# A decode step on one core: the last weight matrix in other pieces, and one early read ahead of the closing add

## The chip, the cores and the metric

The kernel runs on one core of a Trainium2 chip. The metric is the time of one execution in microseconds (us), measured on the device; 212.2 us is the median of four runs of the kernel before (212.13 to 212.42). One of these executions, of 212.18 us, was recorded by the hardware profiler, and every view of the profile below is of that one. The engines are TensorE (PE in the profile; PEld is its loading of weights), VectorE (DVE), ScalarE (ACT), GpSimd (POOL) and SyncE (SP). SP issues nearly all transfers from the chip's memory (HBM) into on-chip memory.

## The reference, cut to what matters

Four tokens of width 576 are normalised; the sum of three things is returned: the tokens, an attention over a window of a long cache, and a multi-layer perceptron.

```python
def _A_ref(x, k_cache, v_cache, wq, wo):       # 4 tokens, 32 query heads, 16 key/value heads of 128
    W = min(4096, max(256, Sk // 4))           # Sk = 8192: the last 2048 positions
    q = (x @ wq) ...                           # by heads
    k, v = the last W rows of the caches, each head used by two query heads
    p = softmax((q . k) * Dh ** -0.5)
    return (p @ v) by tokens @ wo              # wo is 4096 x 576

def _B_ref(x, w1, w2, w3, w4):
    ...                                        # hs: a shift over one position, so it adds zeros
    x1 = x + hs
    h2 = gelu(layernorm(x1) @ w3) @ w4         # w3 is 576 x 4608, w4 is 4608 x 576
    return x1 + h2

xn = layernorm(A_x)
return A_x + _A_ref(xn, ...) + _B_ref(xn, ...)
```

The mixer's four shifts each move the only position out of the sequence, so `w1` and `w2` play no part in the result, and the kernel does not load them.

## The kernel before, in words

**Transfers.** `flush_loads` (L497 to L509) hands SP one list in a fixed order: the keys and values of the 16 heads (2 MB each), four parts of `wo`, `w3` after the values of head 2, and at the very end `w4`. Six buffers hold keys and values, and a transfer is issued when one of them comes free. `w4` is issued by `load_w4` (L135) as six transfers. The 4608 rows of `w4` lie on the 128 partitions as 36 rows of 576 numbers on each (`NF` is 36); the two halves of the matrix give the rows 0 to 17 and 18 to 35 (`NFH` is 18). `W4_PIECES` (L133) cuts these 36 rows: [0, 10, 18, 28, 32, 34, 36], which are pieces of 10, 8, 10, 4, 2 and 2 rows. A row on all partitions is 128 x 1152 bytes, 144 KB.

**The loop.** The big loop (L514 to L565) runs over the heads, with VectorE transposing keys, TensorE making scores and multiplying probabilities with values, and a softmax between them. The first three layers of the perceptron's work lie inside the turn of head 7, so `gT`, its activations, are ready long before the end. The order of the work on each engine is the order in which the code is written.

**The sum of outputs.** Every product with `wo` and with `w4` is accumulated in PSUM by `acc_matmuls` (L177). The width of 576 is cut into two halves of 288 columns (`CW`), which go to different rows of one 8-row sum: the weights, `gT` or `op`, are stored with gaps (`OW` is 10 columns, the tokens in columns 1, 3, 5, 7), and a window of 8 columns beginning at column 1 or at column 0 puts the four tokens on the even or on the odd rows. So a row of `w4` costs two matrix multiplications of 288 columns.

**Two sums at the end.** When the list `second` is filled (L592), every other term is accumulated in another PSUM tile, `acc_odd`, at the rows from 32 on (`QD`), and two multiplications to the two sums run at the same time. `mlp_out(lo, hi)` (L483) takes the rows lo to hi of `w4`, two at a time, one for each sum. After the loop come the last heads' values, the pieces 0 and 1 of `w4`, the last part of `wo`, and the pieces 2 and 3. Then `second` is cleared (L602), ScalarE copies `acc_odd` to `odd` in on-chip memory (L604), the pieces 4 and 5 go to `acc` alone (L605, L606), VectorE adds `acc` and `odd` to `fin` (L609) and SP writes `fin` out (L610).

Of the kernel before, what the change touches and what calls it, by code (L numbers as in the profile page):

```python
# [9 lines left out]
ALU = mybir.AluOpType  # L10
AX = mybir.AxisListType
BF16 = mybir.dt.bfloat16
F32 = mybir.dt.float32
# [9 lines left out]
def kernel(  # L23
# [14 lines left out]
    nc = tc.nc  # L38
    P = 128
    B, Sq, D = A_x.shape  # L40
# [8 lines left out]
    NF = F // P  # L49
    NFH = NF // 2  # L50
# [4 lines left out]
    NQD = P // QD  # L55
    NSL = 4
    SC = NC // NSL
    CW = D // 2
    NW = SC * QD
    assert NW == 512 and NSL * NJ == QD and NQ == 2 * NQD * NW and NFH == 18  # L60
    scale = float(Dh) ** -0.5
# [5 lines left out]
    o2 = out.flatten_outer_dims()  # L67
# [14 lines left out]
    const = ctx.enter_context(tc.tile_pool(name="const", bufs=1))  # L82
# [47 lines left out]
        nc.sync.dma_start(out=t[:, KJ * F:], in_=B_w3[KJ * P:D, :].rearrange("r (e f) -> (r e) f", e=2))  # L130
        w_tiles["w3"] = t

    W4_PIECES = [0, 10, NFH, NFH + 10, NFH + 14, NF - 2, NF]  # L133

    def load_w4():  # L135
        t = wp.tile([P, NF, D], BF16, tag="w", name="w4_sb")
        for lo, hi in zip(W4_PIECES, W4_PIECES[1:]):
            e = lo // NFH
# [8 lines left out]
    ident_f = ident_w[:, 0:P]  # L147
# [7 lines left out]
    def cleared(shape, name):  # L155
        t = const.tile(shape, BF16, name=name)
        flat = t[:] if len(shape) == 2 else t[:].rearrange("p a b -> p (a b)")
        flat = flat.bitcast(F32)
        nc.scalar.activation(out=flat, in_=zero[:].bitcast(F32).to_broadcast(list(flat.shape)), func=ACT.Copy)
        return t  # L160
# [2 lines left out]
    ln2T = cleared([P, KJ + 2, QD], "ln2T")  # L163
    ZP = (NSL - 1) * NJ
    qz = cleared([P, ZP + Hkv * 4 * P], "qz")
    OR = 2 * B
    OW = OR + 2
    gT = cleared([P, NF, OW], "gT")
    op = cleared([P, WOR, OW], "op")

    acc = ps_acc.tile([P, CW], F32)
    nc.vector.memset(acc[:], 0.0)
# [2 lines left out]
    second = []  # L175

    def acc_matmuls(terms):  # L177
        for i in range(2):
            for n, (lhsT, rhs) in enumerate(terms):
                to, q, start = (second[0], QD, second[1]) if second and n % 2 else (acc, 0, False)  # L180
                nc.tensor.matmul(out=to[q:q + OR, :], lhsT=lhsT[:, 1 - i:1 - i + OR],  # L181
                                 rhs=rhs[:, i * CW:(i + 1) * CW], start=start, stop=False, skip_group_check=True)
                if start:
                    second[1] = False
# [43 lines left out]
    for kb in range(NQD):  # L228
        nc.vector.tensor_copy(out=sel[:, :, :, kb, :],
                              in_=ident_bf[:].rearrange("p (ib i e) -> p ib e i", ib=2, e=2))  # L230
# [19 lines left out]
    with nc.allow_low_precision("zeros and ones"):  # L250
# [7 lines left out]
                          in_=sel_j[:].unsqueeze(1).to_broadcast([P, NG, NJ]))  # L258
# [7 lines left out]

    idz = const.tile([B, OW], F32)
    nc.gpsimd.memset(idz[:], 0.0)
    nc.gpsimd.tensor_copy(out=idz[:, 1:OR + 1:2], in_=ident_f[0:B, 0:B])
    xsum = xn_f  # L270
    nc.vector.tensor_tensor(out=xsum[:], in0=xn_f[:], in1=x_bf[:], op=ALU.add)
    acc_matmuls([(idz[:], xsum)])
    ln2_bf = part(D, B)
    layernorm(None, ln2_bf, xn_bf)
# [25 lines left out]
    for r in range(2):  # L300
        nc.vector.tensor_copy(out=q_bf[:, r],
                              in_=qT_ps[:, r].rearrange("p u (g x) -> p g u x", g=NQD)[:, :, :, 0:B])
# [101 lines left out]
    def o_sum(h):  # L404
        oT = st.pop(("oT", h))
        v = oT[:].rearrange("p s (g x) -> p (s g) x", g=NQD)[:, :, 0:NJ].rearrange("p g (b r) -> p b r g", r=rep)
        k = h % WOQ
        if k == 0:
            st["on"] = small.tile([P, WOH, B], BF16, tag="on", name="on")
        with nc.allow_low_precision("summed in float32"):  # L410
            nc.vector.reduce_sum(out=st["on"][:, k * rep:(k + 1) * rep, :].rearrange("p r b -> p b r"),  # L411
                                 in_=v, axis=AX.X)
# [12 lines left out]
    def o_pick(h):  # L425
        if h % WOQ < WOQ - 1:
            return
        R = st.pop("R")
        mk = small.tile([P, WOR, WOH, B], BF16, tag="mk")
        nc.vector.tensor_tensor(out=mk[:], in0=R[:],  # L430
                                in1=own[:].unsqueeze(1).unsqueeze(3).to_broadcast([P, WOR, WOH, B]), op=ALU.mult)
        with nc.allow_low_precision("one term is not zero"):
            nc.vector.reduce_sum(out=op[:, :, 1:OR + 1:2], in_=mk[:].rearrange("p i h b -> p i b h"), axis=AX.X)

    def o_proj(h):
        if h % WOQ < WOQ - 1:
            return
        for i in range(0, WOR, 2):
            acc_matmuls([(op[:, i + u, :], wo_tiles[h // WOQ][:, i + u, :]) for u in range(2)])

    G_CHUNKS = [(e, 4 * g, 4) for e in range(2) for g in range(NQD)] + [(e, 16, 2) for e in range(2)]
    xs = const.tile([P, NF, B], F32, name="g_x")
# [31 lines left out]
    def mlp_act():  # L474
        u = const.tile([P, NF, B], F32, name="g_u")
        nc.vector.tensor_tensor(out=u[:], in0=xs[:], in1=xs[:], op=ALU.mult)
        nc.vector.tensor_scalar(out=u[:], in0=u[:], scalar1=GELU_A, scalar2=1.0, op0=ALU.mult, op1=ALU.add)
        nc.vector.tensor_tensor(out=u[:], in0=u[:], in1=xs[:], op=ALU.mult)
        nc.scalar.activation(out=u[:], in_=u[:], func=ACT.Tanh, scale=GELU_C)
        nc.vector.tensor_scalar(out=u[:], in0=u[:], scalar1=0.5, scalar2=0.5, op0=ALU.mult, op1=ALU.add)  # L480
        nc.vector.tensor_tensor(out=gT[:, :, 1:OR + 1:2], in0=u[:], in1=xs[:], op=ALU.mult)

    def mlp_out(lo, hi):  # L483
        w4 = w_tiles["w4"]
        for i in range(lo, hi, 2):
            acc_matmuls([(gT[:, i + u, :], w4[:, i + u, :]) for u in range(2)])


    order = [("K", 0), ("K", 1), ("K", 2)]
# [24 lines left out]
    for t in range(Hkv):  # L514
        hm, hv, hf, hp = t - 1, t - 2, t - 3, t - 4
        for s in range(NSL):
            if s == NSL - 1 and hm >= 0:
                sm_turn(hm)
            n = t * NSL + s + 1
# [3 lines left out]
            if s == 0:  # L523
                if hm >= 0:
                    sm_max(hm)
                if hv >= 0:
                    sm_rec(hv)
                if hp >= 0:
                    o_pick(hp)
                if hf >= 0:  # L530
                    o_scale(hf)
                k_mask(t)
            elif s == 1 and hm >= 0:
                sm_maxT(hm)
            elif s == 2:
                if hm >= 0:
                    sm_sub(hm)
                    sm_exp(hm)
                if hf >= 0:
                    o_sum(hf)  # L540
            elif s == 3 and hm >= 0:
                sm_den(hm)
# [12 lines left out]
            if t == G_AT:  # L555
                if s < 3:
                    mlp_g(s)
                if s > 0:
                    mlp_turn(s - 1)
                if s == NSL - 1:  # L560
                    mlp_act()
# [27 lines left out]
    o_sum(hl - 1)  # L589
    pieces = list(zip(W4_PIECES, W4_PIECES[1:]))  # L590
    acc_odd = ps_acc.tile([P, CW], F32, tag="g", name="acc_odd")
    second += [acc_odd, True]  # L592
    mlp_out(*pieces[0])
    o_turn(hl)
    o_sum(hl)
    o_spread(hl)
    o_pick(hl)
    mlp_out(*pieces[1])
    o_proj(hl)
    mlp_out(*pieces[2])  # L600
    mlp_out(*pieces[3])
    second.clear()  # L602
    odd = const.tile([OR, CW], F32)
    nc.scalar.activation(out=odd[:], in_=acc_odd[QD:QD + OR, :], func=ACT.Copy)  # L604
    for lo, hi in pieces[4:]:  # L605
        mlp_out(lo, hi)  # L606

    fin = const.tile([OR, CW], out.dtype)
    nc.vector.tensor_tensor(out=fin[:], in0=acc[0:OR, :], in1=odd[:], op=ALU.add)  # L609
    nc.sync.dma_start(out=o2.rearrange("b (i n) -> (b i) n", i=2), in_=fin[:])  # L610


# [28 lines left out]
```

## Time and profile before

| What | Value |
|---|---|
| Median of four runs | 212.2 us (212.13 to 212.42) |
| The profiled execution: its time, its span | 212.18 us, 210.4 us |
| TensorE busy, VectorE busy, ScalarE busy | 150.1, 120.3, 33.9 us |
| Moved from HBM, mean rate over the span | 87.17 MB, 414 GB/s |
| Last piece of `w4` landed | 207.04 us |
| Closing add begins | 207.84 us |
| Mean granted TensorE clock | 0.878 of full speed |

Times in the views are counted from the first instruction. The execution's own time is 1.78 us longer than its span. The chain of waits follows the work that ended last back in time, and names at each step what released it; a line of it is the start, the duration, and the engine with the tile and the line. A row of the timeline is a start, a duration, an engine, the line, the operation, and what it writes and reads; brackets hold the idle time before it and what ended that. The table of stretches gives for each stretch its length, the busy time and count of each engine, the granted clock, the mean busy share of the 16 DMA engines, and the rate in GB/s.

### The profile page before, as it was taken

To read this page: it belongs to the slowest core of one execution; us is meant where nothing else is said; L and a number is where in the kernel's file an instruction comes from. 1 tells how busy PE (TensorE), PEld (TensorE's weight loads), DVE (VectorE), ACT (ScalarE), POOL (GpSimd) and SP (SyncE) were. 2 spreads that over 40 slices of the span, in tenths; PEclk is the share of its full clock that TensorE was granted. 3 is DMA by queue.
4 is the path that set the end of the run, shared out by engine and by line. 5 is a ranking of instruction groups with operands and counts; after the bars stand their busy time and mean duration, and the time that the engine had idled before them with its cause. 6 is when DMAs were issued, how large, how long until landed. Compare 5 with 4: busy or idle time off the path is not lost.

```text
span 210.4 us, 2403 instructions
## 1 busy us (share of the span) xinstructions
PE 150.1 (71%) x955; PEld 62.2 (30%) x955; DVE 120.3 (57%) x216; ACT 33.9 (16%) x64; POOL 2.8 (1%) x15
## 2 busy tenths in 40 slices
PE   0294793889393009769799599987883946988974
PEld 0131231224131003214255143343331321443542
DVE  4732999267730082737504879997578391583220
ACT  7603110021111000202012111220211010202300
POOL 4010000000000000000000000000000000000000
PEclk9999699589978555969699969999999795999999
DMA  7999999999999999999999999999999999999991
GB/s 275 424 392 439 427 428 427 433 433 430 433 442 412 436 430 424 439 430 430 430 430 430 433 422 441 424 430 435 421 435 433 427 430 430 436 424 425 425 407 54
DMA packets 6659, 87.32 MB, mean 415 GB/s; under 512 B 748, under 2 KB 760, under 8 KB 1400
## 3 DMA queue, kind: packets, MB, share of 16 engines
q1 hardware_dynamic: 6640, 87.17, 97.4%
q8 instruction: 7, 0.11, 0.2%
q14 instruction: 4, 0.03, 0.0%
q10 hardware_dynamic: 8, 0.00, 0.0%
HBM read 87.17 MB, written 0.00 MB: 414 GB/s over the span
## 4 chain that ended last, share of the span: by engine, by line
DMA 66%; PE 19%; DVE 7%; issue 4%; ACT 1%; POOL 0%; POOLq 0%; SPq 0%; DVEq 0%
DMA vn<-in_A_v_cache_dram 38%; DMA w_sb<-in_B_w_dram 28%; PE S L336 9%; DVE kt L223 3%; PE g_ps L454 2%; PE O L388 2%; PE q_ps L283 2%; PE acc L181 1%; PE oT L401 1%; DMA first<-in_A_x_dram 1%; PE S L358 1%; DVE qz L315 1%; PE gT_ps L466 1%; DVE mx L342 1%; ACT q_sb L294 1%
## 5 line engine op out<-in xcount | busy, mean ns | idle before, releaser
L223 DVE STREAM_TRANSPOSE kt<-kn 128x1024 int32<-128x1024 int32 x64 | 76.4, 1216 | 10.7 <-DMA kn<-in_A_k_cache_dram 10.6
L336 PE MATMUL S<-kt,qz 128*128 128x512 bf16 x256 | 79.0, 438 | 3.1 <-DVE kt L223 3.1
L388 PE MATMUL O<-vn,PT 128*32 128x512 bf16 x256 | 27.9, 436 | 39.2 <-DMA vn<-in_A_v_cache_dram 38.1
L336 PEld LDWEIGHTS <-qz 128*128 128x128 bf16 x256 | 21.6, 104 | 41.9 <-issue 25.9
L364 ACT ACTIVATE E<-S 128x512 bf16<-128x512 f32 x16 | 9.5, 597 | 119.9 <-PE S L358 119.9
L388 PEld LDWEIGHTS <-PT 128*32 128x32 bf16 x256 | 7.3, 95 | 47.4 <-DVE kt L223 24.9
L370 DVE STREAM_TRANSPOSE PT<-E 128x512 bf16<-128x512 bf16 x16 | 11.4, 710 | 15.4 <-ACT E L364 15.4
L354 DVE TENSOR_REDUCE nm<-mg 8x1 bf16<-8x16 f32 x16 | 2.4, 152 | 23.4 <-PE mg L349 20.7
L395 ACT ACTIVATE O_sb<-O,rd 128x512 f32<-128x512 f32 x16 | 11.0, 686 | 16.3 <-issue 11.0
L342 DVE TENSOR_REDUCE mx<-S 128x1 f32<-128x512 f32 x16 | 10.5, 657 | 1.3 <-PE S L336 1.3
L411 DVE TENSOR_REDUCE on<-oT 128x8 bf16<-128x128 f32 x16 | 4.5, 279 | 10.7 <-PE oT L401 10.7
L401 PE MATMUL oT<-ident_w,O_sb 128*128 128x128 f32 x64 | 10.5, 290 | 0.0
L401 PEld LDWEIGHTS oT<-ident_w,O_sb 128*128 128x128 f32 x64 | 8.5, 152 | 4.5 <-issue 2.3
L181 PE MATMUL acc<-wo_sb,op 128*8 128x288 bf16 x56 | 7.5, 286 | 0.0
L181 PE MATMUL acc<-w_sb,gT 128*8 128x288 bf16 x40 | 5.9, 285 | 1.3 <-DMA w_sb<-in_B_w_dram 1.2
L374 PEld LDWEIGHTS dn<-rs,same_j 128*128 128x128 f32 x32 | 5.8, 188 | 2.9 <-ACT E L364 0.7
L358 PE MATMUL S<-nm,j_row 8*128 8x512 bf16 x16 | 6.6, 410 | 0.0
L327 PE MATMUL S<-negbig,ohT 4*128 4x512 bf16 x16 | 6.2, 385 | 0.0
L349 PE MATMUL mg<-dm,sel_jb 128*8 128x16 bf16 x16 | 2.8, 174 | 3.6 <-DVE dm L344 3.5
L454 PE MATMUL g_ps<-w_sb,ln2T 128*32 128x512 bf16 (+1 forms) x50 | 5.3, 489 | 0.0
L181 PEld LDWEIGHTS <-op 128*8 128x8 bf16 x64 | 4.6, 87 | 2.4 <-issue 0.5
L349 PEld LDWEIGHTS <-sel_jb 128*8 128x8 bf16 x16 | 1.3, 83 | 12.9 <-issue 7.0
(92 smaller groups left out, 79.7 us busy)
## 6 DMA issues: line engine op xcount, KB each, us to landing
kn<-in_A_k_cache_dram SPq DMA_DIRECT2D x16, 2048.0 KB, 22.3
vn<-in_A_v_cache_dram SPq DMA_DIRECT2D x16, 2048.0 KB, 24.9
wo_sb<-in_A_wo_dram SPq DMA_DIRECT2D x4, 1152.0 KB, 25.4
w_sb<-in_B_w_dram SPq DMA_DIRECT2D x1, 4608.0 KB, 35.7
wq_sb<-in_A_wq_dram SPq DMA_DIRECT2D x1, 4096.0 KB, 12.3
w_sb<-in_B_w_dram SPq DMA_DIRECT2D x2, 1440.0 KB, 30.3
w_sb<-in_B_w_dram SPq DMA_DIRECT2D x2, 576.0 KB, 33.4
w_sb<-in_B_w_dram SPq DMA_DIRECT2D x1, 1152.0 KB, 29.9
```

Of the source, the lines that this page charges most:

```text
L181: nc.tensor.matmul(out=to[q:q + OR, :], lhsT=lhsT[:, 1 - i:1 - i + OR], rhs=rhs[:, i * CW:(i + 1) * CW], start=start, stop=False, skip_gro ...
L223: nc.vector.transpose(out=kt[:], in_=src)
L327: nc.tensor.matmul(out=S_ps[h][:].rearrange("p (c k) -> p c k", k=QD), lhsT=ohT[:], rhs=negbig[:].unsqueeze(1).to_broadcast([B, SC, QD]), ...
L336: nc.tensor.matmul(out=S_ps[h][:], lhsT=qz[:, z0:z0 + P], rhs=kt[:, ib, :, e:2 * QD:2].rearrange("p c k -> p (c k)"), start=False, stop=Fa ...
L342: nc.vector.reduce_max(out=mx[:], in_=S_ps[h][:], axis=AX.X)
L358: nc.tensor.matmul(out=S_ps[h][:], lhsT=j_row[:], rhs=st.pop(("nm", h))[:, 0:1].to_broadcast([NJ, NW]), start=False, stop=False, skip_grou ...
L364: nc.scalar.activation(out=E[h][:].rearrange("p c k -> p (c k)"), in_=S_ps.pop(h)[:], func=ACT.Exp, scale=scale, accum_out=rs[:])
L370: nc.vector.transpose(out=PT[h][:], in_=E.pop(h)[:])
L388: nc.tensor.matmul(out=O_ps[h][g * QD:(g + 1) * QD], lhsT=PT[h][:, c, :], rhs=vn[:, :, c, :], start=(s == 0), stop=False, skip_group_check ...
L395: nc.scalar.activation(out=O_sb[h][:], in_=O_ps.pop(h)[:], func=ACT.Copy, scale=st.pop(("rd", h))[:, 0:1])
L401: nc.tensor.transpose(out=oT[:, s, :], in_=o[:, s, :], identity=ident_w[:, s * NJ:s * NJ + P])
L454: nc.tensor.matmul(out=g_ps[g * QD:(g + 1) * QD], lhsT=ln2T[:, k, :], rhs=rhs, start=(j == 0), stop=False, skip_group_check=True)
```

## The change

- The cuts of `w4` become [0, 10, 18, 30, 34, 35, 36]: pieces of 10, 8, 12, 4, 1 and 1 rows, still six transfers.
- `mlp_out` can take a piece of one row. The place where `second` is cleared stays after piece 3, which now ends at row 34 and not 32; so `acc_odd` takes part in two more rows, and the last two rows, one by one, go to `acc` alone.
- After ScalarE's copy to `odd`, VectorE copies one element of `odd` into a new tile `seen` of one number, which nothing reads. The closing add is written as before; it comes after this copy on VectorE.
- Elsewhere the literal 2 for the number of column halves becomes the name `NI`, with the same values: `CW` is 288, `OR` is 8, `OW` is 10, and `ROWS` is the slice from 1 to 9 in steps of 2, as before.

```diff
-    CW = D // 2
+    NI = 2
+    CW = D // NI
...
-    W4_PIECES = [0, 10, NFH, NFH + 10, NFH + 14, NF - 2, NF]
+    W4_PIECES = [0, 10, NFH, NF - 6, NF - 2, NF - 1, NF]
...
-    OR = 2 * B
-    OW = OR + 2
+    OR = NI * B
+    OW = OR + NI
+    ROWS = slice(NI - 1, NI - 1 + OR, NI)
...
     def acc_matmuls(terms):
-        for i in range(2):
+        for i in range(NI):
...
     def mlp_out(lo, hi):
         w4 = w_tiles["w4"]
         for i in range(lo, hi, 2):
-            acc_matmuls([(gT[:, i + u, :], w4[:, i + u, :]) for u in range(2)])
+            acc_matmuls([(gT[:, u, :], w4[:, u, :]) for u in range(i, min(i + 2, hi))])
...
     second.clear()
     odd = const.tile([OR, CW], F32)
     nc.scalar.activation(out=odd[:], in_=acc_odd[QD:QD + OR, :], func=ACT.Copy)
+    seen = const.tile([1, 1], F32)
+    nc.vector.tensor_copy(out=seen[:], in_=odd[0:1, 0:1])
     for lo, hi in pieces[4:]:
         mlp_out(lo, hi)
 
     fin = const.tile([OR, CW], out.dtype)
     nc.vector.tensor_tensor(out=fin[:], in0=acc[0:OR, :], in1=odd[:], op=ALU.add)
```

More of the change, by code (lines that the diff above doesn't have):

```diff
@@ L177, in acc_matmuls @@
     def acc_matmuls(terms):
-        for i in range(2):
+        for i in range(NI):
             for n, (lhsT, rhs) in enumerate(terms):
                 to, q, start = (second[0], QD, second[1]) if second and n % 2 else (acc, 0, False)
-                nc.tensor.matmul(out=to[q:q + OR, :], lhsT=lhsT[:, 1 - i:1 - i + OR],
+                nc.tensor.matmul(out=to[q:q + OR, :], lhsT=lhsT[:, NI - 1 - i:NI - 1 - i + OR],
                                  rhs=rhs[:, i * CW:(i + 1) * CW], start=start, stop=False, skip_group_check=True)
@@ L268 @@
     nc.gpsimd.memset(idz[:], 0.0)
-    nc.gpsimd.tensor_copy(out=idz[:, 1:OR + 1:2], in_=ident_f[0:B, 0:B])
+    nc.gpsimd.tensor_copy(out=idz[:, ROWS], in_=ident_f[0:B, 0:B])
     xsum = xn_f
@@ L432, in o_pick @@
         with nc.allow_low_precision("one term is not zero"):
-            nc.vector.reduce_sum(out=op[:, :, 1:OR + 1:2], in_=mk[:].rearrange("p i h b -> p i b h"), axis=AX.X)
+            nc.vector.reduce_sum(out=op[:, :, ROWS], in_=mk[:].rearrange("p i h b -> p i b h"), axis=AX.X)
     def o_proj(h):
@@ L480, in mlp_act @@
         nc.vector.tensor_scalar(out=u[:], in0=u[:], scalar1=0.5, scalar2=0.5, op0=ALU.mult, op1=ALU.add)
-        nc.vector.tensor_tensor(out=gT[:, :, 1:OR + 1:2], in0=u[:], in1=xs[:], op=ALU.mult)
+        nc.vector.tensor_tensor(out=gT[:, :, ROWS], in0=u[:], in1=xs[:], op=ALU.mult)
     def mlp_out(lo, hi):
@@ L609 @@
     nc.vector.tensor_tensor(out=fin[:], in0=acc[0:OR, :], in1=odd[:], op=ALU.add)
-    nc.sync.dma_start(out=o2.rearrange("b (i n) -> (b i) n", i=2), in_=fin[:])
+    nc.sync.dma_start(out=o2.rearrange("b (i n) -> (b i) n", i=NI), in_=fin[:])
 _INS = ['A_x', 'A_k_cache', 'A_v_cache', 'A_wq', 'A_wo', 'B_x', 'B_w1', 'B_w2', 'B_w3', 'B_w4']
```

## The prediction

> **What bounds the kernel now.** I read the chain of waits first, from its end. Its last links are these (start, duration, what):
>
> ```profile
> 158.41 26.45 DMA vn<-in_A_v_cache_dram
> 184.86 0.02 issue
> 184.88 22.16 DMA w_sb<-in_B_w_dram
> 207.04 0.04 issue
> 207.08 0.66 PE acc L181 x4
> 207.74 0.03 issue
> 207.77 0.02 DVEq L609
> 207.79 0.04 issue
> 207.84 0.45 DVE fin L609
> ```
>
> The last piece of w4 is issued at 184.88 us and lands at 207.04. TensorE needs 0.66 us for its two rows (four multiplications), and 0.10 us pass from TensorE's end at 207.74 to the add. In these 0.10 us stands an instruction of VectorE's queue (DVEq): the add waits for two engines, and the second wait costs an instruction of its own. Up to 207.04 the transfers decide; only the 0.80 us behind that can be worked on by the change.
>
> Next the table of stretches, to see whether the transfers really fill the time before:
>
> ```profile
> 195.00:200.00 5.00, 4.86 (x59) 2.83 (x59) 1.32 (x4) 2.06 (x4) 0.00 (x0) 1.00 1.03 436
> ...
> 204.24:205.00 0.76, 0.72 (x12) 0.56 (x13) 0.00 (x0) 0.00 (x0) 0.00 (x0) 1.00 0.98 391
> 205.00:205.62 0.62, 0.62 (x12) 0.37 (x7) 0.00 (x0) 0.00 (x0) 0.00 (x0) 1.00 0.58 227
> 205.62:206.33 0.71, 0.70 (x10) 0.37 (x8) 0.00 (x0) 0.00 (x0) 0.00 (x0) 1.00 0.50 195
> 206.33:206.70 0.37, 0.33 (x3) 0.25 (x3) 0.00 (x0) 0.34 (x1) 0.00 (x0) 1.00 0.24 93
> 206.70:207.04 0.34, 0.32 (x3) 0.09 (x2) 0.00 (x0) 0.06 (x1) 0.00 (x0) 1.00 0.00 0
> ```
>
> The last two columns are the DMA engines' busy share and GB/s. They are full to 205.0, then fall: some of the 16 engines have finished, the late ones still carry the last pieces. The clock column is 1.00 throughout.
>
> Last the timeline, which shows when TensorE could begin each piece, and the copy and the add:
>
> ```profile
> 204.28 0.28 PE L181 MATMUL acc<-w_sb,gT 128*8 128x288 bf16 x1 [1.19 <-DMA w_sb<-in_B_w_dram]
> ...
> 205.38 0.29 PE L181 MATMUL acc_odd<-w_sb,gT 128*8 128x288 bf16 x1
> 205.66 0.28 PE L181 MATMUL acc<-w_sb,gT 128*8 128x288 bf16 x1
> ...
> 206.03 0.29 PE L181 MATMUL acc_odd<-w_sb,gT 128*8 128x288 bf16 x1
> 206.36 0.40 ACT L604 ACTIVATE odd<-acc_odd 8x288 f32<-8x288 f32 x1 [7.83 <-PE acc_odd L181]
> 206.37 1.36 PE L181 MATMUL acc<-w_sb,gT 128*8 128x288 bf16 x8
> ```
>
> Piece 2 (10 rows) begins at 204.28, piece 3 (4 rows) at 205.66, piece 4 at 206.37, piece 5 at 207.08. Inside piece 2 a pair, one multiplication to each sum, starts every 0.122 us (204.28 to 205.38 in nine steps); the gaps before the later pieces are waits for landings. Taking off the 0.04 us of the chain, the pieces landed at 204.24, 205.62, 206.33 and 207.04.
>
> **The transfers, as they become.** Four rows came 1.38 us after the piece before, two rows 0.71 us. A line through both is 0.335 us a row plus 0.04 us a piece, so one row takes 0.375 us. There are six transfers before and after, with the same bytes and as many packets, so on that line the last landing stays at 207.04. Going back: piece 4 (row 34) lands at 206.67, piece 3 (four rows) at 206.29, piece 2 at 204.91. The price of a packet of one row, 1152 bytes, is not in the trace. Bounds: by bytes alone a row is 0.355 us, and the last landing comes 0.04 us earlier; if a small packet costs what one of two rows costs, each piece takes 0.71 us, and the last landing is 0.67 us later. The far end is a transfer that nothing covers: the tokens' own, four small packets, took 1.57 us in the chain of waits, and two such one behind the other, 3.14 in place of 0.75 us, would land 2.4 us later. I take the line, because the step from four rows to two lay on it almost by bytes, and keep the other ends for the range. The issues cost nothing: SP issues six as before, the last 22 us before its landing. That cover would have to shrink by 22 us before an issue of some 0.4 us showed.
>
> The Trainium skill speaks against such small pieces here: "DMA: Bandwidth & Descriptors", section "Bandwidth", asks for transfers of at least 1 MiB, and its table has 0.95 us for 64 KB and 6.15 us for 1 MB. An estimate between these gives 1.4 us for one row (144 KB) and 2.2 us for two. This trace has 0.71 us for two rows, because the pieces lie queued behind each other and overlap. By the page's table taken one by one, the last two pieces would need 2.8 us and the add would come some 2 us later, at about 214 us; by the trace's row nothing is lost.
>
> **TensorE, as it becomes.** Piece 2 starts at 204.95 and has 12 pairs: 12 x 0.122 = 1.46 us, so TensorE is free at 206.41. Piece 3 has landed (206.29 + 0.04 = 206.33), so its four pairs start at 206.41, 206.53, 206.66 and 206.78; the last ends at 206.78 + 0.29 = 207.07. Piece 4 has two multiplications, at 206.90 and 207.02. Piece 5 is ready at 207.08 but TensorE is free at 207.14: it starts at 207.14 and 207.26 and ends at 207.55. Before, it was 207.74; 0.19 us go, because the last piece has two multiplications in place of four (0.24 us less) and begins 0.06 us late behind the backlog. The total of multiplications is the same, 72. At half clock, which the page shows in earlier slices, every step would double, before and after alike, and TensorE would be the bound in both.
>
> **The copy of the odd sum and the early read.** The price of the longer use of `acc_odd` is that its copy moves back. It began 0.04 us after the last multiplication (206.03 + 0.29 to 206.36); now it begins at 207.11, takes its 0.40 us and ends at 207.51. It had 1.0 us of cover before the add; this cover is now used up. VectorE's early read begins 0.02 us after it (the tanh of the perceptron ended at 118.24 and VectorE went on at 118.26), at 207.53. Nothing else is queued on VectorE behind the waiting read but the add, as its timeline is empty from 201.9 to 207.84; SP's write of the result waits for the add alone. A copy of one element is not in the trace. The nearest row is the smallest copy, 0.136 us (128x16, f32); from below nothing, from above 0.22 us (the copy of 128x128). I take 0.14 us: the read ends at 207.67.
>
> **The add.** It follows a finished instruction of its engine by 0.02 to 0.03 us (117.29 + 0.24 to 117.56), so it begins at 207.70. TensorE's end at 207.55 plus 0.03 us is 207.58, already past. So what the read saves, the queue's instruction (0.07 us of the 0.10), does not show, since the read itself ends last. Behind the add all stays: 0.45 us, the write and its landing. Four more bytes on one partition and one more instruction elsewhere I cost at nothing; no row prices them.
>
> **Sum.** The add begins at 207.70 and not at 207.84: -0.14 us. The profiled execution took 212.18 us, 0.02 under the median of the runs; 212.18 - 0.14 = 212.04 us, rounded to 212.05. The runs shown lie 0.29 us apart, so about 0.2%, 0.42 us, is what a measurement can tell from no change; this gain lies well inside.
>
> **Rivals.**
> 1. TensorE decides: the read costs next to nothing, or piece 3 comes a little earlier. Then the add waits for TensorE alone and begins at 207.58: -0.26 us, 211.92. For it: a copy of one element has less to do than 128x16. Against it: rows of 4x1 and 8x1 also took 0.14 and 0.15 us, so the size hardly counts.
> 2. The change does not do what it says: the add keeps both waits and the queue's instruction behind the read. Then it begins 0.07 us later, at 207.77: -0.07 us, 212.11. For it: before, the link DVEq stands at this add. Against it: VectorE, which works in order, has already waited for ScalarE's copy when it comes to the add. The price is too small to matter for the verdict.
> 3. Slower: packets of one row cost more than the line. The add by TensorE's path begins 0.48 us after the last landing (0.04 + 0.12 + 0.29 + 0.03) once there is no backlog. It reaches 207.84 when the last landing is at 207.36, 0.32 us late: from there on the change loses, and from 0.74 us late it loses over 0.2%. The bound of equal prices, 0.67 us late, gives the add at 208.19: 212.53. The uncovered bound, 2.4 us late, gives 214.26. For it: the rate falls in the last stretches, and no packet of this size was seen. Against it: that fall is from engines that have finished, and four rows and two rows lie on one line.
> 4. Faster by more: the late DMA engines finish earlier. The work left after 205.0 by the shares is 0.58 x 0.62 + 0.50 x 0.71 + 0.24 x 0.37 = 0.80 us of all 16; spread evenly, packets would end near 205.8 and not 206.7. Landings 0.5 us sooner throughout would put the add near 207.2: 211.5. Against it: the change gives every partition the same share as before.
>
> **How the numbers follow.** Chances: the forecast 0.45, rival 1 0.17, rival 2 0.10, rival 3 0.18, rival 4 0.10. The first three all end within 0.2%, but for some 0.03 that a fast landing adds on the faster side and 0.02 on the slower. Of rival 3, 0.15 is beyond 0.2%, of rival 4, 0.09. So faster 0.12, slower 0.17, and 0.71 within. The likeliest one's own range is 211.9 to 212.3. To hold 8 in 10 I go down to 211.75 and up to 212.6, the bound of equal prices; most of rival 4 and the uncovered end of rival 3 are left out.
>
> **What the profile after would show.** Right: pieces begin on TensorE near 204.95, 206.41, 206.90 and 207.14; the copy to `odd` starts near 207.11; a copy of one element of about 0.14 us on VectorE near 207.53; the add near 207.70, with that read or ScalarE, not a queue instruction, ahead of it; the last landing still near 207.04. Wrong: a last landing past 207.36 (rival 3), a wait of the add for TensorE (rival 1), or a DVEq link at the add (rival 2). A whole stream that ends elsewhere, for a reason outside the tail, would make the prediction wrong without any of these steps failing.

## The result, and the profile after

The changed kernel takes 212.04 us (median of 41 runs), the kernel before 212.28 us beside it (61 runs). The ratio is 0.9991, with a 95% interval of 0.9986 to 0.9995: 0.11 to 0.30 us less, 0.19 in the middle. (The mean times lie 0.19 us apart too, the medians 0.24.) The gain is clear of zero, and by the bound of 0.2% it is no change; the forecast was 212.05 us and a change within that bound. The profiled execution took 212.10 us with a span of 210.3 us.

The end of the chain of waits of the changed kernel (start, duration, what):

```profile
205.05 0.04 issue
205.10 0.28 PE acc L183
205.38 0.01 PE acc_odd L183
...
207.10 0.11 PE acc L183
207.22 0.02 PE acc_odd L183
207.24 0.02 issue
207.26 0.41 ACT odd L606
207.67 0.02 issue
207.69 0.14 DVE seen L608
207.84 0.36 DVEq L640
```

Before, the last landing stood in this chain at 207.04. Now the last transfer in it is piece 2, the one of 12 rows, which landed at 205.05. From there TensorE has no pause: 16 pairs, then ScalarE's copy, then the early read. The add itself does not stand in this chain, because it began before the read had ended: the chain goes from the read to an instruction of VectorE's queue at the kernel's end. When the add began is in the timeline.

The timeline of the changed kernel from there (start, duration, engine, line, what it writes and reads; in brackets the idle time before):

```profile
205.10 0.28 PE L183 MATMUL acc<-w_sb,gT 128*8 128x288 bf16 x1 [0.38 <-DMA w_sb<-in_B_w_dram]
...
206.56 0.29 PE L183 MATMUL acc<-w_sb,gT 128*8 128x288 bf16 x1
...
206.94 0.29 PE L183 MATMUL acc_odd<-w_sb,gT 128*8 128x288 bf16 x1
207.05 0.65 PE L183 MATMUL acc<-w_sb,gT 128*8 128x288 bf16 x4
207.26 0.40 ACT L606 ACTIVATE odd<-acc_odd 8x288 f32<-8x288 f32 x1 [7.10 <-PE acc_odd L183]
207.69 0.14 DVE L608 COPY seen<-odd 1x1 f32<-1x1 f32 x1 [4.18 <-ACT odd L606]
207.77 0.43 DVE L613 TENSOR_TENSOR fin<-acc,odd 8x288 bf16<-8x288 f32 x1
208.23 0.37 SPq L614 DMA_DIRECT2D out_dram<-fin  x1
```

The four multiplications of the two single rows begin at 207.05 and end at 207.70; before, TensorE ended at 207.74. The add begins at 207.77 in place of 207.84. In a later profiled execution of the same kernel it began at 207.59: the landings of one execution differ from those of the next by 0.1 to 0.2 us, as much as the change is worth, so a single profile shows which step follows which, and the times of many runs show the sum.

The table of stretches of the changed kernel, for the same stretches as before:

```profile
205.00:205.62 0.62, 0.52 (x10) 0.41 (x11) 0.00 (x0) 0.00 (x0) 0.00 (x0) 1.00 0.65 258
205.62:206.33 0.71, 0.71 (x18) 0.55 (x14) 0.00 (x0) 0.00 (x0) 0.00 (x0) 1.00 0.49 174
206.33:206.70 0.37, 0.37 (x12) 0.31 (x8) 0.00 (x0) 0.00 (x0) 0.00 (x0) 1.00 0.20 69
206.70:207.04 0.34, 0.34 (x10) 0.27 (x5) 0.00 (x0) 0.00 (x0) 0.00 (x0) 1.00 0.03 10
```

The DMA engines' share falls as before, and a little is still moving after 206.70, where before nothing was. TensorE is busy through all the stretches after 205.62.

The two profiled executions differ in one more thing, ahead of the tail. These are the stretches from 186 to 188 us, first before, then after:

```profile
186.00:188.00 2.00, 2.00 (x15) 0.91 (x13) 2.00 (x4) 0.00 (x0) 0.00 (x0) 1.00 0.96 410
186.00:188.00 2.00, 2.00 (x9) 0.39 (x8) 1.51 (x3) 0.00 (x0) 0.00 (x0) 0.50 1.03 442
```

In the second, TensorE was granted half its clock there, and `op`, the last thing that the attention gives to the products with `wo`, was complete at 203.51 us and not at 201.88. TensorE still had to wait 0.38 us for piece 2 (1.19 us before), so the landing decided here too, but with little to spare.

### The profile page after: what moved, and what is told of

Its sections match the earlier page's. It is cut to its first block, busy times and chain, and to the rows that moved or that the text cites. A ratio compares the mean times of both kernels' runs of the same rounds, so it can differ in the third digit from the quotient of the medians.

```text
span 210.3 us, 2403 instructions
## 1 busy us (share of the span) xinstructions
PE 149.9 (71%) x955; PEld 62.6 (30%) x955; DVE 120.6 (57%) x217; ACT 33.9 (16%) x64; POOL 2.8 (1%) x15
## 4 chain that ended last, share of the span: by engine, by line
DMA 68%; PE 19%; DVE 7%; issue 4%; ACT 1%; POOL 0%; POOLq 0%; SPq 0%; DVEq 0%
DMA w_sb<-in_B_w_dram 33%; DMA vn<-in_A_v_cache_dram 24%; DMA wo_sb<-in_A_wo_dram 10%; PE S L338 7%; PE acc L183 3%; DVE kt L225 3%; PE g_ps L456 2%; PE q_ps L285 2%; PE O L390 1%; PE oT L403 1%; DMA first<-in_A_x_dram 1%; DVE qz L317 1%; PE gT_ps L468 1%; DVE mx L344 1%; PE S L360 0%
## 5 line engine op out<-in xcount | busy, mean ns | idle before, releaser
L390 PE MATMUL O<-vn,PT 128*32 128x512 bf16 x256 | 27.2, 425 | 40.6 <-DMA vn<-in_A_v_cache_dram 36.6
L403 PE MATMUL oT<-ident_w,O_sb 128*128 128x128 f32 x64 | 11.1, 302 | 0.0
L403 PEld LDWEIGHTS oT<-ident_w,O_sb 128*128 128x128 f32 x64 | 9.1, 160 | 4.9 <-issue 3.1
L183 PE MATMUL acc<-w_sb,gT 128*8 128x288 bf16 x38 | 5.1, 286 | 0.4 <-DMA w_sb<-in_B_w_dram 0.4
L474 DVE COPY g_x<-gT_ps 128x64 f32<-128x64 f32 (+1 forms) x3 | 0.6, 195 | 7.7 <-PE gT_ps L468 7.7
```

The costliest lines, as they stand in the source:

```text
L183: nc.tensor.matmul(out=to[q:q + OR, :], lhsT=lhsT[:, NI - 1 - i:NI - 1 - i + OR], rhs=rhs[:, i * CW:(i + 1) * CW], start=start, stop=False ...
L390: nc.tensor.matmul(out=O_ps[h][g * QD:(g + 1) * QD], lhsT=PT[h][:, c, :], rhs=vn[:, :, c, :], start=(s == 0), stop=False, skip_group_check ...
L403: nc.tensor.transpose(out=oT[:, s, :], in_=o[:, s, :], identity=ident_w[:, s * NJ:s * NJ + P])
```

## The experiments

Theory A is that of the prediction: the gain is the shorter work behind the last landing (two multiplications and not four), less what the later copy of the odd sum takes back. Theory B is that the gain comes from the early read. Theory C is that only the landings count.

**The read alone.** The changed kernel with the old pieces:

```diff
-    W4_PIECES = [0, 10, NFH, NF - 6, NF - 2, NF - 1, NF]
+    W4_PIECES = [0, 10, NFH, NFH + 10, NFH + 14, NF - 2, NF]
```

> The pieces are those of the kernel before (10, 8, 10, 4, 2, 2); only VectorE's early read of one element is added. Theory A (the gain comes from the shorter work behind the last landing): the copy to odd still ends about 1 us ahead of the add, so the read is hidden, and only the queue's instruction goes: the add begins 0.03 to 0.07 us after TensorE's end and not 0.10, so -0.05 us, ratio 0.9998. Theory B (the gain comes from the read): -0.2 us, ratio 0.9991, as the whole change. Theory C (the gain comes from transfers that land sooner): 0.

Measured: 212.17 us, ratio 0.9997 (0.9988 to 1.0006). The end of its chain of waits:

```profile
206.91 0.04 issue
206.95 0.66 PE acc L183 x4
207.62 0.02 issue
207.64 0.45 DVE fin L613
```

There is no instruction of VectorE's queue any more, and the add follows TensorE's end by 0.02 us in place of 0.10. So the read does what it is made for, and it is worth about 0.07 us where it is covered: it ran at 206.66, almost 1 us ahead of the add. The add itself began 0.20 us earlier than before, but 0.13 of that is a landing at 206.91 and not 207.04, which this execution happened to have. The time fits 0.07 us and cannot tell it from nothing; nor does it exclude the whole gain of the change, 0.9991, which lies inside the interval.

**The pieces alone.** The changed kernel without the read:

```diff
-    seen = const.tile([1, 1], F32)
-    nc.vector.tensor_copy(out=seen[:], in_=odd[0:1, 0:1])
```

> The changed kernel without the early read; pieces 10, 8, 12, 4, 1, 1. Theory A: the copy to odd and TensorE end within 0.05 us of each other, so the add begins about 0.10 us after the later one, with a queue instruction (DVEq) ahead of it, within 0.05 us of where it begins in the changed kernel: -0.15 to -0.2 us against the kernel before, ratio 0.9992. Theory B: the gain is gone, ratio 1.000. Theory C: ratio 0.9991.

Measured: 212.10 us, ratio 0.9992 (0.9984 to 1.0001). Its chain of waits ends so:

```profile
207.13 0.50 PE acc L183 x4
207.63 0.03 issue
207.65 0.02 DVEq L611
207.67 0.04 issue
207.72 0.45 DVE fin L611
```

The queue's instruction is back, and the gain is still there to within 0.0001 of the changed kernel's. Theory B would have lost it all; as the interval reaches 1.0001, the time alone does not exclude that, and the profiles have to decide (see the longer read). The copy to odd ended at 207.57 here (207.17 + 0.40), TensorE at 207.63: the two ends lie side by side, as the prediction had it.

**A longer last piece.** Twice: the kernel before with its last two pieces made one of 4 rows, once with five transfers, once with six (there rows 18 to 27 come in two pieces, of 4 and 6).

```diff
-    W4_PIECES = [0, 10, NFH, NFH + 10, NFH + 14, NF - 2, NF]
+    W4_PIECES = [0, 10, NFH, NFH + 10, NFH + 14, NF]            # five transfers
+    W4_PIECES = [0, 10, NFH, NFH + 4, NFH + 10, NFH + 14, NF]   # six; second is cleared after piece 4
```

> The kernel before with its last two pieces of 2 rows made one of 4 (10, 8, 10, 4, 4; five transfers). Theory A: eight multiplications and not four lie behind the last landing, 4 x 0.122 = 0.49 us more, less 0.04 us for the piece that is gone: +0.45 us, ratio 1.0021, and in the profile 1.15 us from the last landing's release to TensorE's end. Theory B says nothing of it. Theory C (landings decide, the work behind them does not): -0.04 us or nothing, ratio 1.000.

> As the kernel before, but with pieces of 10, 8, 4, 6, 4, 4 rows: the last piece has 4 rows as in the run with five transfers, and there are six transfers again. In that run the add began 0.55 us later than before, but the time grew by 0.87 us. If the rest was the number of transfers (SyncE's waits at the end of the program fall differently), this run shows only the multiplications: +0.49 us, ratio 1.0023, and from the add's start to the end of the span 2.56 us as before. Rival: the rest belongs to the last piece of 4 rows itself: ratio 1.004 again.

Measured: with five transfers 213.07 us, ratio 1.0041 (1.0027 to 1.0055); with six 212.68 us, ratio 1.0025 (1.0015 to 1.0035). The chain of waits with six transfers:

```profile
207.00 0.04 issue
207.04 1.15 PE acc L181 x8
208.19 0.03 issue
208.22 0.02 DVEq L610
208.24 0.04 issue
208.28 0.45 DVE fin L610
```

The last landing is where it was (207.00), TensorE needs 1.15 us behind it and not 0.66, and the time grows by 0.53 us. That is theory A's term, the multiplications behind the last landing, doubled in place of halved, and clear of the noise; theory C is out. With five transfers the time grew by 0.34 us more. There the add began at 208.39, but the span ended at 211.5, 3.1 us behind it, where it was 2.56 us before; with six transfers again it is 2.57. The rest thus comes with the number of transfers and lies behind the add (last section).

**A longer read.** The changed kernel, with all of odd read:

```diff
-    seen = const.tile([1, 1], F32)
-    nc.vector.tensor_copy(out=seen[:], in_=odd[0:1, 0:1])
+    seen = const.tile([OR, CW], F32)
+    nc.vector.tensor_copy(out=seen[:], in_=odd[:])
```

> The changed kernel, but VectorE copies all of odd (8 x 288) into seen and not one element. Theory A with the step of the prediction that the chain copy to odd, early read, add is the one that ends last: the read of one element took 0.14 us and let the add begin 0.08 us after it; 288 elements a row should take 0.3 to 0.45 us (the closing add of the same shape took 0.44), so the add begins 0.15 to 0.35 us later than in the changed kernel, and the gain is gone: ratio to the kernel before 0.9995 to 1.0008. Rival: TensorE ends last and covers the read: the time stays that of the changed kernel, 0.9991.

Measured: 212.14 us, ratio 0.9996 (0.9987 to 1.0005). Its timeline:

```profile
206.98 0.65 PE L183 MATMUL acc<-w_sb,gT 128*8 128x288 bf16 x4
207.19 0.40 ACT L606 ACTIVATE odd<-acc_odd 8x288 f32<-8x288 f32 x1 [8.47 <-PE acc_odd L183]
207.62 0.30 DVE L608 COPY seen<-odd 8x288 f32<-8x288 f32 x1 [5.55 <-ACT odd L606]
207.85 0.44 DVE L613 TENSOR_TENSOR fin<-acc,odd 8x288 bf16<-8x288 f32 x1
```

TensorE ended at 207.63, and the add waited until 207.85 behind the read: 0.23 us after the read's start, against 0.08 in the changed kernel. In the profile the read is on the path, so lengthening it moves the add by 0.15 us. In the time it shows as about half of the gain lost, at the lower edge of what was expected, and the intervals of the two kernels overlap; by the time alone this is not settled.

Counting from the start of piece 2 on TensorE, from which it has no pause in any of these kernels, takes the scatter of the landings out. The add began 2.67 us after it in both profiled executions of the changed kernel (205.10 to 207.77, 204.92 to 207.59), 2.72 us without the read (205.00 to 207.72) and 2.83 us with the long read (205.02 to 207.85). So in the changed kernel the read is worth 0.05 us, not the whole gain, and making it longer costs 0.16 us: theory B is out by the profiles.

**Seven transfers.** Rows 32 to 35 in pieces of 2, 1, 1, and acc_odd closed after row 31, as before; then the same with rows 32 and 33 also in both sums.

```diff
-    W4_PIECES = [0, 10, NFH, NF - 6, NF - 2, NF - 1, NF]
+    W4_PIECES = [0, 10, NFH, NF - 8, NF - 4, NF - 2, NF - 1, NF]
...
     mlp_out(*pieces[3])
+    mlp_out(*pieces[4])            # the second kernel alone; the last rows are then pieces[5:]
```

> Seven pieces, 10, 8, 10, 4, 2, 1, 1, with the early read; acc_odd takes part up to row 32 as in the kernel before. Theory A: the copy to odd is back at about 206.4 us and hidden, no backlog stands on TensorE, the last piece has two multiplications: last landing 207.04 + 0.04 for a seventh piece, + 0.04 + 0.12 + 0.29 + 0.03, add at 207.56 and not 207.84: -0.28 us against the kernel before, ratio 0.9987, 0.1 us faster than the changed kernel. Theory B: as the changed kernel, 0.9991. Theory C: as the changed kernel or slower, if a small piece costs more than 0.04 us.

> Seven transfers of 10, 8, 10, 4, 2, 1, 1 rows with the early read, as in the run with seven transfers before, but the piece of rows 32 and 33 goes to both sums and the copy to odd comes after it. Theory A: TensorE has no backlog; copy to odd at 206.82 to 207.22, read at 207.25; the last row begins at the last landing and TensorE ends 0.45 us after it, near 207.49; add at 207.52, -0.32 us. Behind the add the run with seven transfers needed 2.70 us and not 2.56 to the end of the span; if that belongs to the number of transfers, it is so here too, and the gain against the kernel before is -0.18 us, ratio 0.9991; if not, 0.9985.

Measured: 212.06 us, ratio 0.9991 (0.9982 to 1.0000), and 212.13 us, ratio 0.9996 (0.9987 to 1.0005). Both missed the add they were to have, 207.56 and 207.52. The first one's chain of waits:

```profile
206.39 0.04 issue
206.44 1.17 PE acc L183 x8
207.60 0.02 issue
207.62 0.45 DVE fin L613
```

Eight single multiplications without a pause: with one sum alone four rows cost 1.17 us, which keeps TensorE busy until the last row has landed. The trace also records each landing. The last row landed at 207.14 in the first kernel and at 207.21 in the second, where 207.04 to 207.08 was expected, and 0.48 us from the landing to the add give 207.62 and 207.69, as measured. So both missed by a later landing and not by the work behind it. And in both the span ended 2.7 us behind the add, 0.1 us more than with six transfers. Neither beats the changed kernel.

**Another cut with six transfers.** Pieces of 10, 8, 11, 4, 2, 1 rows, the copy to odd again well ahead of the add; run twice, the second time beside the changed kernel on the same chip.

```diff
-    W4_PIECES = [0, 10, NFH, NF - 6, NF - 2, NF - 1, NF]
+    W4_PIECES = [0, 10, NFH, NF - 7, NF - 3, NF - 1, NF]
```

> Six transfers of 10, 8, 11, 4, 2, 1 rows, with the early read; acc_odd takes part up to row 33. Theory A: the copy to odd ends near 207.2 and is hidden; TensorE has its last rows back to back and ends near 207.61 or 207.49 (at the last landing, 207.04, plus 0.45); the add follows by 0.02: at 207.52 to 207.63, -0.2 to -0.3 us against the kernel before, ratio 0.9986 to 0.9990. Theory B (only the read counts): as the changed kernel, 0.9991.

> The changed kernel itself, beside the run with 10, 8, 11, 4, 2, 1 rows on the same chip: ratio 0.9991 to the kernel before, as in its result.

> Pieces of 10, 8, 11, 4, 2, 1 rows with the early read, beside the changed kernel on the same chip. Theory A: the copy to odd is hidden and the last piece has two multiplications, so 0.05 to 0.1 us faster than the changed kernel: ratio to the kernel before 0.9987. Rival: the copy and the read never cost anything that shows in the time: the same as the changed kernel.

Measured: 211.95 us, ratio 0.9988 (0.9979 to 0.9997); then the changed kernel 211.96 us, ratio 0.9990 (0.9981 to 0.9999), and beside it this cut 212.04 us, ratio 0.9992 (0.9984 to 1.0001). So it is not faster than the changed kernel, against theory A's expectation. The add began at 207.78 in the first profile and at 207.69 in the second, where 207.52 to 207.63 was expected. Its second profile shows why, in the last links of the chain of waits:

```profile
206.75 0.91 PE acc L183 x6
207.66 0.02 issue
207.69 0.45 DVE fin L613
```

The read was long done (at 207.23 + 0.14), but three rows go to one sum, at twice TensorE's price a row, from the landing of the two-row piece on. The last row landed at 207.08, so that without a backlog the add would have come at 207.56: the backlog cost 0.13 us. What the hidden copy saves, TensorE spends. In the changed kernel run beside it the add began at 207.59.

**The price of a piece of one row.** The last ten rows one by one to acc alone, so that TensorE waits for each landing; and the same rows in five pieces of two.

```diff
-    W4_PIECES = [0, 10, NFH, NF - 6, NF - 2, NF - 1, NF]
+    W4_PIECES = [0, 10, NFH] + list(range(NF - 10, NF + 1))       # ten pieces of one row
+    W4_PIECES = [0, 10, NFH] + list(range(NF - 10, NF + 1, 2))    # five of two
...
-    mlp_out(*pieces[3])            # in both: second is cleared after piece 2; the last rows are pieces[3:]
```

> Ten pieces of one row at the end (10, 8, 8 and ten times 1; 13 transfers); acc_odd takes part up to row 26, so the ten last rows go one by one to acc alone, two multiplications each, 0.24 us, and TensorE waits for every landing. The time from row to row in the trace is the price of a piece of one row. The prediction's line: 0.375 us, ten rows in 3.75 us, last landing some 0.3 us later than before for seven more pieces. Bytes alone: 0.355. Equal price for small and large packets: 0.71 us a row, the last landing 3.4 us later. The time itself also has SyncE's other end of the program with 13 transfers in it, and is no price of the pieces.

> As the run with ten pieces of one row, but the last ten rows in five pieces of 2 (8 transfers). On the line: 0.71 us from piece to piece, five in 3.55 us, 0.2 us less than in the other run for the same rows. If pieces of one row cost more than the line, the difference is larger.

Measured: 212.22 us, ratio 1.0007 (0.9997 to 1.0017), and 212.51 us, ratio 1.0014 (1.0004 to 1.0024). The timeline of TensorE's weight loads, and the end of the chain, with ten pieces of one row:

```profile
206.61 0.21 PEld L183 LDWEIGHTS <-gT 128*8 128x8 bf16 x2 [0.15 <-issue]
206.99 0.21 PEld L183 LDWEIGHTS <-gT 128*8 128x8 bf16 x2 [0.17 <-issue]
207.37 0.08 PEld L183 LDWEIGHTS <-gT 128*8 128x8 bf16 x1 [0.17 <-issue]
...
207.79 0.02 issue
207.81 0.45 DVE fin L612
```

The last three rows begin 0.38 us apart, where the line had 0.375; equal prices would have been 0.71. The last landing is near 207.33 (207.37 less 0.04), 0.29 us later than before, for seven more pieces; the line gave 0.28. With it the add begins at 207.81, 0.48 us behind the last landing, the figure that the prediction had worked out for a piece of one row without a backlog. (These pieces were issued later too, as a transfer waits for an earlier one: SyncE issued until 205.14. The 0.38 us by itself is therefore an upper bound for pieces that are queued long before.) The changed kernel's own landing records close this gap, for its two single rows were issued some 22 to 27 us before they landed. Its last three pieces landed at 206.45, 206.80 and 207.16, and in the second profiled execution at 206.27, 206.63 and 207.00: 0.35 to 0.37 us for a piece of one row.

In the run with pieces of two, TensorE did not wait for the last ten rows: it came to them at 205.61, when two of the five pieces had landed, and ran 20 multiplications without a pause (2.61 us). Its landings, at 203.75, 204.45, 205.20, 205.92 and 206.62 for piece 2 and the four after it, give 0.70 to 0.75 us for a piece of two rows, where the line has 0.71. This profile is of the slowest of the eight executions (212.81 us); in it TensorE was granted half its clock from 186 to 188 us, and `op` was complete at 203.60.

## Why the prediction was right

**What bounds the kernel.** Right for the kernel before: the transfers decide up to the last landing, and more work behind it lengthened the time. In the changed kernel the chain no longer comes from the last landing but from that of piece 2, with 2.67 us of work behind it. And TensorE's idle time ahead of piece 2 is not always there. In three of the fourteen profiled executions (the changed kernel's first, the second of 10, 8, 11, 4, 2, 1 rows, the one with pieces of two) the granted clock was 0.50 from 186 to 188 us and `op` was complete 1.6 us later than in the other eleven, at 203.5 to 203.6 in place of 201.8 to 202.1. In the first of these 0.38 us of idle time were left. In the second none shows, though TensorE still began piece 2 right behind its landing (landed at 204.59, begun at 204.63). In the third piece 2 had landed at 203.75 and TensorE came to it only at 204.63: there the attention decided, and not the transfers.

**The transfers, the line.** Right: in every kernel whose last one-row pieces were issued long before, the landing records give 0.35 to 0.39 us for such a piece; the line had 0.375, and equal prices would have been 0.71. The Trainium skill's table in "DMA: Bandwidth & Descriptors", section "Bandwidth", which is of transfers issued from GpSimd and from which an estimate of 1.4 us was worked out for such a piece, does not hold for these pieces, queued behind each other by SyncE: the measured row decides. The landing of a whole execution, however, is not a constant: piece 2 came at 205.05 in the one profiled execution and at 204.88 in the other, against 204.91 predicted. The last row landed at 207.16 and at 207.00, against 207.04 predicted; so the two small pieces moved the last landing by no more than the executions differ.

**TensorE.** Right in its order and its durations: pieces at 205.10, 206.56, 207.05 and, without a pause, the last row 0.24 us on, each 0.15 us later than predicted, all by the landing of piece 2. The backlog behind the piece of 12 rows is there, and it is why the last row's landing has left the chain. That the multiplications behind the last landing are the term that counts is shown for a longer last piece by the run with four rows and six transfers: +0.53 us measured, +0.49 expected. For a shorter one the profile with ten pieces of one row shows it: 0.48 us from the last landing to the add, and not 0.80. In the changed kernel only a part of these 0.32 us is won, because the backlog and the copy stand behind the last landing in their place.

**The copy and the read.** Right that the copy's cover of 1 us is used up and that the read ends last by a hair: copy to 207.66, read from 207.69 to 207.83, TensorE's end at 207.70. Mis-sized was one term: the add was put 0.02 to 0.03 us behind the read's end, but VectorE began it 0.08 us after the read's start, 0.06 us before its end. The read of one element took 0.142 us, as taken from the smallest copy; on the path it costs only 0.08. So what the read saves shows after all, where the prediction had held that it does not: counted from piece 2, the add comes 0.05 us sooner with the read than without it. The row used, one instruction 0.02 us behind another, came from operations that each need the result of the one before; the add does not need the read's. The profile before already had rows of the other kind. Here the reciprocal, which does not need `dm`, begins 0.09 us before the end of `dm`:

```profile
100.68 0.23 DVE L344 TENSOR_SCALAR dm<-sel_g,mx 128x16 bf16<-128x16 bf16 x1
100.82 0.16 DVE L379 RECIPROCAL rd<-dn 128x1 f32<-128x1 f32 x1
```

That the need for the result makes the difference fits all these rows; no run changed that alone. With 0.08 us the add should have been put at 207.61, or 0.23 us earlier than before, where the ratio of the times has 0.19 (0.11 to 0.30) and the forecast had 0.14.

**The sum.** That 212.05 was forecast and 212.04 measured is in part luck. The forecast gain of 0.14 us came out as 0.19, and the kernel before was measured at 212.28 us in place of the 212.18 from which the sum went. In the profiled execution two misses also partly cancelled each other: the landing of piece 2 came 0.14 us late, and the add began 0.09 us sooner after the read's start than the sum had it.

**Rivals.** Rival 2 did not happen (no queue instruction at the add). Rival 1, TensorE deciding, is nearly as true as the forecast: by TensorE's end alone the add would have begun at 207.72 (0.02 us behind 207.70, as in the run with the read alone), 0.05 us before it did, and the times cannot tell the two apart. Rival 3 did not happen: the last landing, at 207.16 and 207.00, came before 207.36. Rival 4 did not happen either: piece 2 landed 0.14 us late and 0.03 us early, not half a microsecond early.

## What to carry to other kernels

When a kernel waits for one long stream of transfers, what can still be won at its end is the work behind the last landing: cut the last piece so that little is left to do with it, and check that the pieces ahead of it leave no backlog and that what was hidden under the old last piece (here a copy) still ends in time. Check too how much idle time the engine has ahead of the last pieces, and in more than one profile; here 0.38 us, or none, was left when TensorE's granted clock had fallen to half some 17 us before. The floor of such a tail can be worked out before trying: landing, wait, the last piece's own work, the closing step; here about 0.3 us of 212 (0.80 less 0.48). Other cuts of the same rows only moved the same tenths between TensorE, the copy and the end of the program, so once the bound's own scatter is as large as what is left, stop.

## What the runs showed of the hardware that was not expected

Taking one transfer out of the program made its end longer. From the add's start to the end of the span it took 2.55 to 2.58 us in every profile with six pieces of `w4`, 3.08 us with five, 2.70 and 2.71 with seven (two kernels), 2.77 with eight and 2.62 with thirteen, though the add, the write of 4.5 KB and the kernel's code behind it are the same. SyncE's own waits for the write at the end of the program differ; first the kernel before, then the one with five transfers (waited in total, times, longest):

```profile
SPq L636 <- DMA out_dram<-fin: 0.2, 1, 0.2
```

```profile
SPq L636 <- DMA out_dram<-fin: 0.7, 1, 0.7
```

With seven and with thirteen pieces this wait is 0.7 us too, and with eight 0.8, though with thirteen the end is hardly longer than with six. So the wait alone does not explain it, and the cause is open. What stands is the size: a change in the number of transfers can move the end by 0.05 to 0.5 us without touching the work, and it has to be held constant when a few tenths are compared.

VectorE began an instruction that does not need the result of the one before it 0.06 to 0.07 us ahead of that one's end (the add behind the read of one element at 207.77, the read ending at 207.83; behind the long read at 207.85, which ended at 207.92).

The parts of one transfer do not land together. Each transfer reports its landing in 16 parts. Of the last piece before, eight had landed by 205.74 us, and the other eight landed from 206.54 to 207.04; in the changed kernel it was eight by 205.74 and eight from 206.60 to 207.16. That fits the way in which the prediction read the falling share of the DMA engines. No run evened them out, and what that would gain stays open.
